# Interleaved attention and feed-forward on one core: the score tiles of VectorE moved, side work paused around them, six key tiles in column groups instead of eight

## The chip, the cores and the metric

The kernel runs on one core of a Trainium2 chip. The metric is the device time of one execution in microseconds (us). Before the change it is 2252.2 us, the median of three runs (2249.78 to 2252.49). Engines are named as in the profile: PE is the matrix engine, PEld its weight loads, DVE the vector engine, ACT the scalar engine, POOL GpSimd, SP the sync engine.

## What is computed

Two layers of attention and two of feed-forward, in turn, with the same weights in both rounds, on 2048 rows of 512 columns:

```python
x = x + _A_ref(_layernorm(x), A_wqkv, A_wo)
x = x + _B_ref(_layernorm(x), B_w1, B_w2)
x = x + _A_ref(_layernorm(x), A_wqkv, A_wo)
x = x + _B_ref(_layernorm(x), B_w1, B_w2)
```

`_A_ref` is full softmax attention with 32 heads of 16 dimensions: scores of 2048 by 2048 for each head, softmax over the keys, the weighted sum of the values, a product with `wo`. `_B_ref` is `silu(x @ w1) @ w2` with 1792 hidden columns. There is no mask, so every head needs all of its 4.2 million exponentials in each layer.

## The kernel before

**Units.** In a layer (`L`), the 2048 queries are four chunks of 512 (`c`), the 32 heads are eight groups of four (`hb`), and the 2048 keys are sixteen tiles of 128 (`kt`). One unit is (`c`, `hb`, `kt`): four heads, 512 queries, 128 keys. I call the sixteen units of one (`c`, `hb`) a block; a layer has 32 blocks, the kernel 64. PE, ACT and DVE each run in the order in which the program emits instructions; POOL and SP follow their own queues.

**What a unit emits** (lines 671 to 759). First the exponentials: a unit's scores lie in two PSUM tiles of 128 by 1024 (`s_ps`, two heads each, "pair 0" and "pair 1"), and ACT turns each into `p_sb` (line 686). Then PE gets the score products of the next unit (`emit_s`, four products of 32 rows that lie in different row groups, line 555). Then come the products of probabilities and values (`emit_pv`) that were put off by the unit before, then those of this unit's pair 0, and last the side work. The `s_ps` tiles are a ring of three, so a score product waits for the exponential three tiles back.

**Values in two forms.** For key tiles in `COL` the four heads' value products are 32 columns wide and go to four column groups (line 570). For the others, `DIAG`, each head's values lie in their own 32 of 128 columns of a zeroed tile `vd`, and four products of full width add up in `o_ps` (line 580). POOL fills the `vd` tiles, two key tiles at a time in a ring of two (`vd_fill`, line 151), from the value tensor `va`. Value products of a `COL` tile are put off whole to the next unit; of a `DIAG` tile, pair 1 is put off. At `kt` 0 both pairs are put off, because `o_ps` has one buffer and has to be emptied first (`finish_heads`, line 659, a DVE copy to `oT`).

**DVE's score tiles.** At key tiles in `OFF`, pair 1's exponential is made by DVE in seven passes (`exp_passes`, line 589). The first, `split` (line 601), reads the `s_ps` tile and is emitted in the unit itself; the other six are emitted one per unit in the following units. Until `split` has run, its `s_ps` tile isn't free. The value products of this pair are emitted seven units later (`late`).

**Side work.** Everything else is cut into steps that a queue (`Pump`) hands out at the end of a unit: for chunk 0 the key projections of the next head group (`k_piece`, steps a and b of two products each, four pieces, and `amax_bm`), for every block the query projection of the next block (`q_piece`, steps a, b, d) and the transposition of the finished heads (`heads_piece`), and for chunks 1 to 3 the previous chunk's output projection (`epilogue_pieces`: pa | pb, pc, four times), layer norm (`ln_steps`: statistics in two steps, then rs, then four transpositions tr), feed-forward (`ffn_pieces`: a, b, d for each of 14 hidden tiles, d being ACT's tanh with a DVE product; then 28 steps of the second product) and in layer 0 the next layer's layer norm and values (`next_pieces`). All side work on PE shares one PSUM buffer (`gpool`, one buffer, tile tag "g"): a step that opens a new tile waits until DVE has read the last one.

**How many steps.** Before the change a unit takes the queue's length, with a little for what the coming blocks will add, divided by the units left in the chunk, and rounded up; at least one while the next block's projections wait; none at `OFF` (lines 746 to 754). At `kt` 14 it takes as many as the next block's query needs. The number `left` is never set back, so in practice at least one step is taken in every unit up to `kt` 13 while the queue holds something.

**Ahead of the loop**: layer norm of all rows, the first projections, and on POOL the filling of constants: `va` is set to 1.0 throughout (line 142), because column 17 of each head must be one (it makes the softmax sum), and the weight columns are rearranged (line 125).

Of the kernel before, what the change touches and what calls it, by code (L numbers as in the profile page):

```python
# [18 lines left out]
def kernel(  # L19
# [10 lines left out]
    nc = tc.nc  # L30
# [15 lines left out]
    EPS = 1e-5  # L46
    VS = DH + 1
    NG = 2
    NR = 2

    COL = [1, 3, 5, 7, 9, 11, 13, 15]
    DIAG = [kt for kt in range(TT) if kt not in COL]

    KR = 32

    OFF = [1, 9]

    cpool = ctx.enter_context(tc.tile_pool(name="cpool", bufs=1))
    wpool = ctx.enter_context(tc.tile_pool(name="wpool", bufs=1))
# [57 lines left out]
    wkq = wpool.tile([P, CT, 2 * D + DH], BF16, name="wkq")  # L117
# [20 lines left out]
    VW = VS * H + 32 - VS  # L138
    vs = []
    for i in range(2):  # L140
        va = xpool.tile([P, TT, VW], BF16, name=f"va{i}")
        nc.gpsimd.memset(va[:], 1.0)
        vs.append(va)
    vdq = []
    for i in range(NR):
# [2 lines left out]
        vdq.append(vd)  # L148


    def vd_fill(va, hb, g, slot):
        k0, step = DIAG[NG * g], DIAG[1] - DIAG[0]
        for j in range(4):
            h = 4 * hb + j
            nc.gpsimd.tensor_copy(  # L155
                out=vdq[slot][:, :, j, 32 * j : 32 * j + VS],
                in_=va[:, k0 : k0 + step * (NG - 1) + 1 : step, VS * h : VS * h + VS],
            )


    def ln_stats(mvb, i, tt):
        st = small.tile([P, 6], FP32, name="st", tag="st")
# [110 lines left out]
    def amax_bm(hb):  # L273
        if OFF:
            ends = KT[64:P, hb, :].rearrange("p (k n) -> p k n", n=P)
# [266 lines left out]
    pump = Pump()  # L542
    state = {"begun": False}

    def pump_some(n):
        for _ in range(n):
            if not pump.q:
                return
            state["begun"] = pump.step()
# [11 lines left out]
            )  # L561
        return s_ps

    def emit_pv(o_ps, ps, hb, kt, prs, va):
        for pr in prs:
            for jj in range(2):
                j = 2 * pr + jj
                if kt in COL:
                    h = 4 * hb + j
                    nc.tensor.matmul(  # L570
                        o_ps[32 * j : 32 * j + 32, :],
                        lhsT=va[:, kt, VS * h : VS * h + 32],
                        rhs=ps[pr][:, jj, :],
                        start=False,
                        stop=(kt == TT - 1),
                        skip_group_check=True,
                    )
                else:
                    d = DIAG.index(kt)
                    nc.tensor.matmul(  # L580
                        o_ps[:, :],
                        lhsT=vdq[d // NG % NR][:, d % NG, j, :],
                        rhs=ps[pr][:, jj, :],
                        start=(kt == 0 and j == 0),
                        stop=False,
                        skip_group_check=True,
                    )
# [48 lines left out]
    for L in range(2):  # L636
        va = vs[L]
        last = L == 1
        QTs = [[None] * HB for _ in range(NQC)]
# [5 lines left out]
            for tt in range(0, TT, 2):  # L645
                v_two(xnTs[tt // 4], tt, va)
        for i in range(NR):
            vd_fill(va, 0, i, i)
# [8 lines left out]
        left = 0  # L657

        def finish_heads(o_ps, hb, attn):
            oT = opool.tile([P, 512], BF16, name="oT", tag="oT")  # L660
# [10 lines left out]
        for u, (c, hb, kt) in enumerate(units):  # L671
# [3 lines left out]
            off = kt in OFF  # L675

            ps = []
# [22 lines left out]
            if kt == 0:  # L700
                flush(u)
                assert not late
                if o_ps is not None:
                    finish_heads(o_ps, (hb - 1) % HB, attn)
                if hb == 0:
                    if c > 0:
                        pump.add(epilogue_pieces(c - 1, attn))
                        pump.add(ffn_pieces(c - 1, emit_out=last))
                        if not last:
                            pump.add(next_pieces(c - 1, nxt, vs[1]))  # L710
                    attn = new_attn
                o_ps = oppool.tile([P, 512], FP32, name="o_ps", tag="o")
                pend.append((o_ps, ps, hb, kt, (0, 1)))
                must = []
                if c == 0 and hb + 1 < HB:
                    must += [k_piece(xnTs, k, hb + 1) for k in range(NQC)]
                    must.append([lambda hb=hb: amax_bm(hb + 1)])
                if hb + 1 < HB:
                    must.append(q_piece(xnTs, c, hb + 1, QTs))
                elif c + 1 < NQC:  # L720
                    must.append(q_piece(xnTs, c + 1, 0, QTs))
                at = (1 if state["begun"] else 0) + (1 if u > 0 else 0)
                pump.q[at:at] = [list(p) for p in must]
                left = at + len(must)
            else:
                flush(u)
                if off:
                    s_now += [f() for f in nxt_s[1:]]
                    emit_pv(o_ps, ps, hb, kt, (0,), va)
                    late.append((u + 7, (o_ps, ps, hb, kt, (1,))))  # L730
                elif kt in COL:
                    pend.append((o_ps, ps, hb, kt, (0, 1)))
                else:
                    emit_pv(o_ps, ps, hb, kt, (0,), va)
                    pend.append((o_ps, ps, hb, kt, (1,)))
# [24 lines left out]
        flush(len(units) + TT)  # L760
        finish_heads(o_ps, HB - 1, attn)
# [36 lines left out]
```

## Time and profile before

| what | value |
|---|---|
| median of three runs | 2252.2 us |
| the profiled execution's own time | 2250.19 us |
| its span, first to last instruction | 2248.0 us |
| mean granted PE clock | 0.927 |
| PE, DVE, ACT, POOL busy | 1904.9, 1495.2, 1849.0, 354.5 us |
| exponentials on ACT (line 686) | 1920, busy 1806.0 us, idle 263.0 us before them |
| value products, full width (line 580) | 2048 |
| value products, column groups (line 570) | 1792 with `p_sb`, 256 with `pd_sb` |

A line of the instruction groups reads: source line, engine, operation, what it writes and reads with shapes, count, then busy time in us and the mean of one in ns, then the engine's idle time just before these instructions with what ended it. Times of single instructions overlap: ACT's exponentials last 1086 ns each but start 0.905 us apart when nothing holds them.

### The profile page before, as it was taken

Reading aid. Unit: us, or ns where it says so; the run is one execution under the profiler, and the core shown is the slowest. Engines: PE = TensorE matmul, PEld = TensorE weight load, DVE = VectorE, ACT = ScalarE, POOL = GpSimd, SP = SyncE. Lnnn points to the kernel's source line nnn. Section 1 sums busy time; section 2 is a strip of 40 time slices with the busy share of each in tenths; the row PEclk is TensorE's granted clock in tenths of the full one; section 3 lists DMA queues with packets and bytes.
Section 4 is the critical chain, followed back from the end, with each engine's and each line's share of the span. In section 5 each row is a group of like instructions: output and inputs, shape, how many; then the busy total and the mean of one; then the engine's idle time right before and its main releaser. Section 6 shows DMA issues by size and latency. Waiting matters only on the chain.

```text
span 2248.0 us, 29378 instructions
## 1 busy us (share of the span) xinstructions
PE 1904.9 (85%) x10560; PEld 590.5 (26%) x10560; DVE 1495.2 (67%) x2023; ACT 1849.0 (82%) x2024; POOL 354.5 (16%) x1048
## 2 busy tenths in 40 slices
PE   2989887888888987889867888898899888988896
PEld 1322222222222222222222222222223222322222
DVE  7676767666666666666745767667666766676664
ACT  0688887998789987999814888899999899999991
POOL 4111111121111211111100111112122121212210
PEclk9998899999899998999977989899999899999997
DMA  4000000000000000000000000000000000000000
GB/s 140 1 1 1 1 1 1 1 1 1 1 1 1 1 1 1 1 1 1 1 0 0 1 1 1 1 1 1 1 6 6 1 1 3 8 1 1 1 10 10
DMA packets 8481, 11.82 MB, mean 5 GB/s; under 512 B 400, under 2 KB 7312, under 8 KB 8336
## 3 DMA queue, kind: packets, MB, share of 16 engines
q1 hardware_dynamic: 7280, 8.39, 1.1%
q8 instruction: 82, 1.34, 0.3%
q10 hardware_dynamic: 1056, 1.57, 0.2%
q14 instruction: 63, 0.52, 0.1%
HBM read 7.86 MB, written 2.10 MB: 4 GB/s over the span
## 4 chain that ended last, share of the span: by engine, by line
PE 59%; ACT 18%; DVE 18%; issue 5%; DMA 0%; ACTq 0%; DVEq 0%
PE s_ps L555 19%; PE o_ps L580 17%; ACT p_sb L686 15%; PE o_ps L570 8%; PE y_ps L433 3%; PE h_ps L426 3%; DVE y L596 3%; PE k_ps L239 2%; ACT t_sb L463 2%; PE q_ps L327 2%; DVE st L163 2%; DVE amax L281 2%; PE y_ps L405 1%; DVE oT L661 1%; PE v_ps L290 1%
## 5 line engine op out<-in xcount | busy, mean ns | idle before, releaser
L686 ACT ACTIVATE p_sb<-s_ps 128x1024 bf16<-128x1024 f32 x1920 | 1806.0, 1086 | 263.0 <-PE s_ps L555 258.6
L555 PE MATMUL s_ps<-QT,KT 32*128 32x512 bf16 x4096 | 695.6, 400 | 140.0 <-ACT p_sb L686 113.9
L580 PE MATMUL o_ps<-p_sb,vd 128*128 128x512 bf16 x2048 | 645.6, 404 | 6.4 <-DVE oT L661 6.4
L155 POOL COPY vd<-va 128x34 bf16<-128x34 bf16 x1024 | 331.2, 337 | 1813.7 <-PE o_ps L580 1667.1
L555 PEld LDWEIGHTS <-KT 32*128 32x128 bf16 x4096 | 185.0, 91 | 777.7 <-issue 712.2
L596 DVE SCALAR_TENSOR_TENSOR y<-y,m 128x1024 f32<-128x1024 f32 x256 | 313.5, 1225 | 4.0
L570 PE MATMUL o_ps<-p_sb,va 128*32 128x512 bf16 x1792 | 215.4, 410 | 1.0 <-ACT p_sb L686 0.8
L580 PEld LDWEIGHTS <-vd 128*128 128x128 bf16 x2048 | 126.4, 99 | 272.6 <-issue 260.4
L601 DVE TENSOR_SCALAR z<-s_ps 128x1024 int32<-128x1024 f32 x128 | 155.9, 1218 | 21.6 <-PE s_ps L555 20.9
L596 DVE SCALAR_TENSOR_TENSOR pd_sb<-y,z 128x1024 bf16<-128x1024 f32 x128 | 158.4, 1237 | 3.7
L596 DVE SCALAR_TENSOR_TENSOR y<-m 128x1024 f32<-128x1024 f32 x128 | 156.0, 1219 | 0.0
L464 DVE SCALAR_TENSOR_TENSOR hT<-t_sb,h_ps 128x512 bf16<-128x512 f32 x84 | 57.6, 686 | 121.2 <-ACT t_sb L463 121.2
L661 DVE CAST oT<-o_ps 128x512 bf16<-128x512 f32 x64 | 44.3, 692 | 135.8 <-PE o_ps L570 135.8
L426 PE MATMUL h_ps<-xnT,w_sb 128*128 128x512 bf16 x448 | 130.6, 397 | 2.8 <-DVE hT L511 1.4
L433 PE MATMUL y_ps<-w_sb,hT 128*128 128x512 bf16 x448 | 123.8, 384 | 7.0 <-DVE hT L511 4.5
L208 PE MATMUL t_ps<-ident,xn 128*128 128x128 bf16 x256 | 34.8, 286 | 92.3 <-DVE xn L196 88.7
L342 DVE TENSOR_SCALAR qc<-q_ps,cols 128x512 bf16<-128x512 f32 x64 | 51.8, 809 | 84.8 <-PE q_ps L327 84.8
L256 DVE TENSOR_SCALAR KT<-k_ps,cols 128x512 bf16<-128x512 f32 x56 | 45.4, 810 | 92.0 <-PE k_ps L239 91.9
L327 PE MATMUL q_ps<-xnT,wkq 128*128 128x512 bf16 x256 | 79.6, 397 | 14.6 <-DVE attn L377 14.6
L607 DVE TENSOR_SCALAR m<-z 128x1024 int32<-128x1024 int32 x128 | 88.8, 694 | 4.4
L613 DVE TENSOR_SCALAR z<-z 128x1024 int32<-128x1024 int32 x128 | 88.1, 688 | 1.8
L570 PEld LDWEIGHTS <-va 128*32 128x32 bf16 x2048 | 55.0, 94 | 129.3 <-issue 129.0
(64 smaller groups left out, 998.2 us busy)
## 6 DMA issues: line engine op xcount, KB each, us to landing
w_sb<-in_B_w_dram SPq DMA_DIRECT2D x2, 1792.0 KB, 14.9
x_sb<-in_A_x_dram SPq DMA_DIRECT2D x4, 512.0 KB, 9.7
out_dram<-x_sb SPq DMA_DIRECT2D x16, 128.0 KB, 1.7
wraw<-in_A_wqkv_dram ACTq DMA_DIRECT2D x1, 1024.0 KB, 7.5
wv_sb<-in_A_wqkv_dram ACTq DMA_DIRECT2D x1, 512.0 KB, 10.0
wo_sb<-in_A_wo_dram SPq DMA_DIRECT2D x1, 512.0 KB, 11.9
```

The lines of the kernel that those rows point to most:

```text
L155: nc.gpsimd.tensor_copy(out=vdq[slot][:, :, j, 32 * j : 32 * j + VS], in_=va[:, k0 : k0 + step * (NG - 1) + 1 : step, VS * h : VS * h + VS],)
L327: nc.tensor.matmul(cell["ps"][:, :], lhsT=wkq[:, ct, P * hb + DH : P * hb + DH + P], rhs=xnTs[c][:, ct, :], start=(ct == 0), stop=(ct == C ...
L426: nc.tensor.matmul(ps, lhsT=w1_sb[:, ct, ft * P : (ft + 1) * P], rhs=xfT[:, ct, :], start=(ct == 0), stop=(ct == CT - 1),)
L433: nc.tensor.matmul(ps, lhsT=hT[:, ft, tq * P : (tq + 1) * P], rhs=w2_sb[:, ft, :], start=(ft == 0), stop=(ft == FT - 1),)
L555: nc.tensor.matmul(s_ps[:, jj, :], lhsT=KT[32 * j : 32 * j + KR, hb, kt * P : (kt + 1) * P], rhs=QT[32 * j : 32 * j + KR, :], start=True, ...
L570: nc.tensor.matmul(o_ps[32 * j : 32 * j + 32, :], lhsT=va[:, kt, VS * h : VS * h + 32], rhs=ps[pr][:, jj, :], start=False, stop=(kt == TT ...
L580: nc.tensor.matmul(o_ps[:, :], lhsT=vdq[d // NG % NR][:, d % NG, j, :], rhs=ps[pr][:, jj, :], start=(kt == 0 and j == 0), stop=False, skip ...
L596: nc.vector.scalar_tensor_tensor(out=out, in0=in0, scalar=POLY[k], in1=in1, op0=ALU.add, op1=ALU.mult)
L601: nc.vector.tensor_scalar(out=z[:], in0=s_ps[:].rearrange(flat), scalar1=-127.5 / (SCALE * LOG2E), scalar2=float(SCALE * LOG2E * 2**23), o ...
L607: nc.vector.tensor_scalar(out=m[:].bitcast(I32), in0=z[:], scalar1=0x7FFFFF, scalar2=0x3F800000, op0=ALU.bitwise_and, op1=ALU.bitwise_or,)
L613: nc.vector.tensor_scalar(out=z[:], in0=z[:], scalar1=0x40000000, scalar2=0x7F800000, op0=ALU.bitwise_xor, op1=ALU.bitwise_and,)
L686: nc.scalar.activation(p_sb[:].rearrange("p a b -> p (a b)"), s_now[pr][:].rearrange("p a b -> p (a b)"), ACT.Exp, scale=float(SCALE),)
```

## The change

- `COL` goes from the eight odd key tiles to `[2, 5, 7, 9, 12, 14]`, so `DIAG` has ten tiles, 0, 1, 3, 4, 6, 8, 10, 11, 13, 15, in five groups of two. `vd_fill` takes a running number of the group; the ring of two `vd` tiles stays.
- `OFF` goes from `[1, 9]` to `[2, 9]`.
- `REST` is the key tiles 0, 1, 2, 8, 9. There no side step is taken. Eleven of sixteen units take steps where fourteen did.
- The number of steps is reckoned over the units that are not in `REST`, with 4 steps (13 in chunk 0) for each coming block, and separately over the units up to `kt` 14 for the pieces that the next block needs (`due`); the larger counts. The rule of at least one step is gone.
- `va` is no longer filled whole: only the ones column of each head is set to 1.0, and the 15 columns of padding to 0.0. The weight columns are rearranged in another order of the same eight copies.

```diff
-    COL = [1, 3, 5, 7, 9, 11, 13, 15]
+    COL = [2, 5, 7, 9, 12, 14]
     DIAG = [kt for kt in range(TT) if kt not in COL]
+    GROUPS = [DIAG[i : i + NG] for i in range(0, len(DIAG), NG)]
 
-    OFF = [1, 9]
+    OFF = [2, 9]
+
+    REST = sorted({0} | {kt - 1 for kt in OFF} | set(OFF))
...
-    for ct in range(CT):
-        pairs = wkq[:, ct, 0 : 2 * D].rearrange("p (h t d) -> p h t d", t=2, d=DH)
-        for t in range(2):
+    for t in range(2):
+        for ct in range(CT):
+            pairs = wkq[:, ct, 0 : 2 * D].rearrange("p (h t d) -> p h t d", t=2, d=DH)
...
-        nc.gpsimd.memset(va[:], 1.0)
+        heads = va[:, :, 0 : VS * H].rearrange("p t (h s) -> p t h s", s=VS)
+        nc.gpsimd.memset(heads[:, :, :, DH:VS], 1.0)
+        nc.gpsimd.memset(va[:, :, VS * H : VW], 0.0)
...
-    def vd_fill(va, hb, g, slot):
-        k0, step = DIAG[NG * g], DIAG[1] - DIAG[0]
+    def vd_fill(va, at):
+
+        at_hb, g = divmod(at, len(GROUPS))
+        k0, k1 = GROUPS[g]
         for j in range(4):
-            h = 4 * hb + j
+            h = 4 * (at_hb % HB) + j
             nc.gpsimd.tensor_copy(
-                out=vdq[slot][:, :, j, 32 * j : 32 * j + VS],
-                in_=va[:, k0 : k0 + step * (NG - 1) + 1 : step, VS * h : VS * h + VS],
+                out=vdq[at % NR][:, :, j, 32 * j : 32 * j + VS],
+                in_=va[:, k0 : k1 + 1 : k1 - k0, VS * h : VS * h + VS],
             )
...
-                left = at + len(must)
+                due = pump.q[at + len(must) - 1] if must else None
...
-            nd = len(DIAG)
             if kt in DIAG and DIAG.index(kt) % NG == 0 and u > 0:
-                at_d = (c * HB + hb) * nd + DIAG.index(kt) + NG * (NR - 1)
-                if at_d < NQC * HB * nd:
-                    fhb, fd = at_d // nd % HB, at_d % nd
-                    vd_fill(va, fhb, fd // NG, fd // NG % NR)
-
-            remaining = TT * HB - (hb * TT + kt)
-            total = pump.steps()
-            later = sum(3 for _ in range(hb + 1, HB)) + (HB - 1 - hb)
-            todo = -(-(total + later) // remaining) if total else 0
-            if left and kt < TT - 2 and pump.q:
-                todo = max(todo, 1)
-            if off:
-                todo = 0
-            pump_some(todo)
+                at = (c * HB + hb) * len(GROUPS) + DIAG.index(kt) // NG + NR - 1
+                if at < NQC * HB * len(GROUPS):
+                    vd_fill(va, at)
+
+            if kt not in REST:
+                here = sum(1 for k in range(kt, TT) if k not in REST)
+                rest = here + (TT - len(REST)) * (HB - 1 - hb)
+                later = (HB - 1 - hb) * (4 + (9 if c == 0 else 0))
+                todo = -(-(pump.steps() + later) // rest) if pump.q else 0
+                where = [i for i, p in enumerate(pump.q) if p is due]
+                if where:
+                    steps = sum(len(p) for p in pump.q[: where[0] + 1])
+                    slots = sum(1 for k in range(kt, TT - 1) if k not in REST)
+                    todo = max(todo, -(-steps // max(slots, 1)))
+                pump_some(todo)
             if kt == TT - 2:
-
-                tgt_c, tgt_hb = (c, hb + 1) if hb + 1 < HB else (c + 1, 0)
-                while tgt_c < NQC and QTs[tgt_c][tgt_hb] is None:
+                while any(p is due for p in pump.q):
                     pump_some(1)
```

More of the change, by code (lines that the diff above doesn't have):

```diff
@@ L562, in emit_s, with emit_pv @@
         return s_ps
-    def emit_pv(o_ps, ps, hb, kt, prs, va):
+    def emit_pv(o_ps, ps, c, hb, kt, prs, va):
         for pr in prs:
@@ L578, in emit_pv @@
                 else:
-                    d = DIAG.index(kt)
+                    g, i = divmod(DIAG.index(kt), NG)
+                    at = (c * HB + hb) * len(GROUPS) + g
                     nc.tensor.matmul(
                         o_ps[:, :],
-                        lhsT=vdq[d // NG % NR][:, d % NG, j, :],
+                        lhsT=vdq[at % NR][:, i, j, :],
                         rhs=ps[pr][:, jj, :],
@@ L647 @@
         for i in range(NR):
-            vd_fill(va, 0, i, i)
+            vd_fill(va, i)
         nxt = [None] * NQC
@@ L656 @@
         s_now = [emit_s(QTs[0][0], 0, 0, pr) for pr in range(2)]
-        left = 0
+        due = None
         def finish_heads(o_ps, hb, attn):
@@ L712 @@
                 o_ps = oppool.tile([P, 512], FP32, name="o_ps", tag="o")
-                pend.append((o_ps, ps, hb, kt, (0, 1)))
+                pend.append((o_ps, ps, c, hb, kt, (0, 1)))
                 must = []
@@ L728 @@
                     s_now += [f() for f in nxt_s[1:]]
-                    emit_pv(o_ps, ps, hb, kt, (0,), va)
-                    late.append((u + 7, (o_ps, ps, hb, kt, (1,))))
+                    emit_pv(o_ps, ps, c, hb, kt, (0,), va)
+                    late.append((u + 7, (o_ps, ps, c, hb, kt, (1,))))
                 elif kt in COL:
-                    pend.append((o_ps, ps, hb, kt, (0, 1)))
+                    pend.append((o_ps, ps, c, hb, kt, (0, 1)))
                 else:
-                    emit_pv(o_ps, ps, hb, kt, (0,), va)
@@ L735 @@
-                    pend.append((o_ps, ps, hb, kt, (1,)))
+                    emit_pv(o_ps, ps, c, hb, kt, (0,), va)
+                    pend.append((o_ps, ps, c, hb, kt, (1,)))
             if passes and not off:
                 passes.pop(0)()
-            nd = len(DIAG)
             if kt in DIAG and DIAG.index(kt) % NG == 0 and u > 0:
-                at_d = (c * HB + hb) * nd + DIAG.index(kt) + NG * (NR - 1)
-                if at_d < NQC * HB * nd:
-                    fhb, fd = at_d // nd % HB, at_d % nd
-                    vd_fill(va, fhb, fd // NG, fd // NG % NR)
```

## The prediction

> **What bounds it now.** I read the page first.
>
> ```profile
> span 2248.0 us, 29378 instructions
> PE 1904.9 (85%) x10560; PEld 590.5 (26%) x10560; DVE 1495.2 (67%) x2023; ACT 1849.0 (82%) x2024; POOL 354.5 (16%) x1048
> ...
> L686 ACT ACTIVATE p_sb<-s_ps 128x1024 bf16<-128x1024 f32 x1920 | 1806.0, 1086 | 263.0 <-PE s_ps L555 258.6
> ...
> L155 POOL COPY vd<-va 128x34 bf16<-128x34 bf16 x1024 | 331.2, 337 | 1813.7 <-PE o_ps L580 1667.1
> ```
>
> ACT's exponentials are the floor, and the 258.6 us in which they waited for score products are all there is to win. In the timeline an undisturbed unit takes 1.81 us (two exponentials), a unit in `OFF` 0.905. A block's floor is 14 x 1.81 + 2 x 0.905 = 27.15 us; eight blocks, 217.2. The windows of the chunks (layer 0 chunks 0 and 1, layer 1 chunks 0 and 1; first number the length, last but two the PE clock):
>
> ```profile
> 73.50:329.60 256.10, 223.78 (x1198) 63.52 (x1198) 181.58 (x208) 223.49 (x241) 34.40 (x126) 0.91 0.00 1
> 329.60:592.00 262.40, 224.40 (x1290) 69.36 (x1288) 173.15 (x246) 231.43 (x256) 40.54 (x128) 0.95 0.00 1
> ...
> 1210.50:1470.00 259.50, 227.62 (x1199) 63.67 (x1193) 180.66 (x206) 223.79 (x240) 34.40 (x126) 0.88 0.00 1
> 1470.00:1710.00 240.00, 217.17 (x1256) 66.62 (x1254) 163.11 (x213) 229.59 (x255) 47.48 (x128) 0.96 0.01 3
> ```
>
> Above the floor: chunk 0, 38.9 and 42.3 us; chunks 1 to 3, 45.6 on average in layer 0 (45.2, 48.4, 43.2) but 22.8 in layer 1. Before each exponential I noted the wait. In a late block of chunk 0 (ACT alone, last figure the idle time before):
>
> ```profile
> 234.01 2.85 ACT L686 ACTIVATE p_sb<-s_ps 128x1024 bf16<-128x1024 f32 x3 [1.44 <-PE s_ps L555]
> 238.71 1.02 ACT L686 ACTIVATE p_sb<-s_ps 128x1024 bf16<-128x1024 f32 x1 [1.84 <-PE s_ps L555]
> 241.07 12.94 ACT L686 ACTIVATE p_sb<-s_ps 128x1024 bf16<-128x1024 f32 x14 [1.34 <-PE s_ps L555]
> 254.55 11.11 ACT L686 ACTIVATE p_sb<-s_ps 128x1024 bf16<-128x1024 f32 x12 [0.55 <-PE s_ps L555]
> ```
>
> The waits lie at the block's end (the query is late), at key tiles 1 and 2, and at 9. Units with one side step elsewhere wait for nothing. Layer 0's chunks 1 to 3 pay most in block 0, the one block whose units take two steps: 42.7, 46.8, 43.5 us against 32.1, 29.1, 29.1 in layer 1, where they take one.
>
> PE's prices at full clock, as distances of starts:
>
> ```profile
> 1220.51 0.40 PE L570 MATMUL o_ps<-p_sb,va 128*32 128x512 bf16 x4
> 1220.84 0.61 PE L580 MATMUL o_ps<-p_sb,vd 128*128 128x512 bf16 x2
> 1221.28 0.59 PE L239 MATMUL k_ps<-xnT,wkq 128*128 128x512 bf16 x2
> 1221.81 0.60 PE L555 MATMUL s_ps<-QT,KT 32*128 32x512 bf16 x4
> 1222.34 0.61 PE L580 MATMUL o_ps<-p_sb,vd 128*128 128x512 bf16 x2
> ```
>
> Column groups 0.33 us a key tile, full width 2 x 0.44 = 0.88, a unit's scores 0.53, a side step 0.44. A step that opens the shared PSUM tile after a step that DVE must still read waits (layer 0, chunk 1, block 0):
>
> ```profile
> 344.02 0.59 PE L405 MATMUL y_ps<-wo_sb,aT 128*128 128x512 bf16 x2
> 344.65 0.69 DVE L417 TENSOR_TENSOR x_sb<-x_sb,y_ps 128x512 bf16<-128x512 bf16 x1 [1.20 <-PE y_ps L405]
> 345.39 0.38 PE L396 MATMUL a_ps<-ident,attn 128*128 128x128 bf16 x4 [0.78 <-DVE x_sb L417]
> ```
>
> **The change, part by part.** Below, a unit's PE work is the sum of these prices; PE may run about 1.1 us late before ACT waits: a score product can start 1.1 us after a unit's first exponential, when the tile three back is free.
>
> *Key tiles at full width.* 64 blocks x 2 x (0.88 - 0.33) = 70 us more PE time. A block then needs 16 x 0.53 + 10 x 0.88 + 6 x 0.33 = 19.3 us and 0.44 per side step; with 11 steps 24.1, under the floor, so ACT covers it; with 22 steps 29.0, not covered: it is in the sums below. POOL makes 256 more `vd` copies (86 us at 337 ns); each fill has about three units (5.4 us) for four copies, and POOL idled 1813.7 us before them. If that cover failed, 1.3 us a fill would show.
>
> *`OFF` and rests.* An `OFF` unit lasts 0.905, so the next scores come late by what PE does between. At tile 9 with an unpumped tile 8 before it the trace has 0.36 (units where the queue was empty), with 0.97 us of value products between (0.33 + 0.20 + 0.44); with a step, 0.78 to 0.81. After, 0.77 us lies there: 0.15. At tile 2 it is 0.88 + 0.44 = 1.32: 0.36 + 0.35 = 0.7. Tile 1 costs nothing. So 0.9 a block where single steps suffice, for 1.7 to 3 now: the gain.
>
> *Where the steps go.* By the new formula chunk 0's blocks 1 to 5 take two steps at tiles 3 to 7 and 10, one at 11. Chunks 1 to 3 begin with 121 steps (layer 1) or 137 (layer 0) for 88 units; two a unit until 121 - 2n <= 88 - n: 33 units (three blocks), in layer 0 49 (four and a half). Then one.
>
> *Chunk 0, blocks 1 to 5.* [heads, k0a] at tile 3: the trace's [heads, qa] at tile 2 cost 0.52 to 0.55: 0.5. [k0b, k1a], [k1b, k2a], [k2b, k3a] at 4, 5, 6: each time PE waits for DVE's 0.81 us copy, about 0.9 by the 0.78 above. PE 0.53 + 0.88 + 0.88 + 0.9 = 3.2 at tile 4, 2.75 at 5, 3.1 at 6, less 1.81 each: 3.6, I take 3.3. Nearest rows, [pc, pa]: 0.65 to 1.75. Then `amax_bm` runs at tile 7, on DVE:
>
> ```profile
> 191.60 0.29 DVE L278 TENSOR_SCALAR KT<-KT,cols 64x256 bf16<-64x256 bf16 x1
> 191.93 2.29 DVE L281 TENSOR_REDUCE amax<-KT 128x1 f32<-128x2048 bf16 x1
> 194.25 0.25 DVE L285 TENSOR_SCALAR Bm<-E,amax 128x128 bf16<-128x128 bf16 x1
> ```
>
> Behind the last K copy come these 2.8 us, the pass of tile 8 (1.24) and only then `split` of tile 9 (1.22), which holds a score tile. In order: k3b ends 0.9 us after tile 8's first exponential; copy to 1.9, amax to 4.7, pass to 5.95, `split` to 7.2; scores 0.4: tile 11 starts at 7.7 instead of 4.7: 3.0. Before, amax lay at tile 11, far from a `split`. Bounds: 0 (DVE catches up) to 4.1 (all of amax and the pass). PE idles 3.2 us there. In this trace the clock fell to 0.50 behind smaller waits of PE (1.36 us for the query, at 199.74):
>
> ```profile
> 199.00:202.00 3.00, 2.27 (x14) 0.56 (x16) 1.81 (x3) 1.78 (x2) 0.52 (x2) 0.74 0.00 0
> 202.00:205.00 3.00, 2.21 (x13) 0.57 (x8) 1.34 (x4) 1.16 (x3) 0.00 (x0) 0.50 0.00 0
> ```
>
> so the two pumped units behind it (1.85 us of PE work each) run at half clock, each about 1 us over: 2.0 more (0 to 4). The block's-end wait (1.7) goes, the query being ready by tile 11. Sum 0.7 + 0.5 + 3.3 + 3.0 + 2.0 = 9.5 against 5.9 now. Block 0: 6 (no K waits); block 6 (amax at tile 10, after `split`): 4.7; block 7: 0.9. Chunk 0: 6 + 47.5 + 4.7 + 0.9 = 59; less 38.9 and 42.3: **+37**.
>
> [...]
>
> *Chunks 1 to 3.* Block 0: 0.7; [heads, qa] 0.6; [qb, qd] 1.5 (rows 0.82 to 2.38); output projection, [pa, pb] 0.6 and [pc, pa] 1.0 twice, 3.3; [rs, tr0] 5.0 (row 4.51; 0.7 us more of passes lie ahead on DVE); [tr1, tr2] 1.4 (row 1.36 to 1.78): 12.4, say 12. Blocks 1 and 2, feed-forward: [a, b], [d, a], [b, d]. In [b, d] tanh sits in ACT's queue behind a b just issued; the row at tile 10 is 1.16, of which 0.48 is tanh itself. In [d, a] PE waits for tanh and DVE's 0.69 and passes the delay to b. I take 1.2 per triple, 3.6 a block, beside tanh 0.48 each: 9.7 and 8.8 with heads, query and tile 2. Layer 0 then 5.7, 3.5 ([y, y] pairs cost 0.01 in their rows) and three times 0.9: 42.4 against 45.6, three times: **-10**. Layer 1 then 2.4 and four times 0.9: 36.5 against 22.8, three times: **+41**.
>
> *The rest.* Between the layers and at the tail the order is the same. The `va` fills were 15.3 us of POOL ahead of `vd`, while PE's and DVE's first work runs until 73.5 us; POOL waited 36.1 us for DVE there: 0, and no cost if slower, up to that wait.
>
> Sum 37 - 10 + 41 = 68. On the profiled execution's 2250.19: 2318; the median lies 2.0 higher: **2320 us**.
>
> **The rivals.**
> *Faster: the waits hide.* Some 186 units hold a PE wait inside a pair (4 in each of twelve chunk 0 blocks, about 25 in each other chunk of layer 0, 21 in layer 1). I price them near 0.9. If they cost 0.5 (lowest rows: 0.51, 0.52), -0.4 x 186 = -74: 2246. It decides below 0.55. For it: [st0, st1] and [a, b] cost nothing. Against: the ten other [pa, pb] and [pc, pa] units, 0.65 to 1.75.
> *amax meets no `split`.* 12 blocks x 5.0 = -60: 2260. For it: DVE is 70% busy in chunk 0's window. Against: its queue is in order.
> *Half clock spreads.* The chunk 0 windows already run at 0.88 to 0.91. Another 2 us in 12 blocks and 3 in six layer norms: +42, 2362.
>
> **How the numbers follow.** Chances: forecast 0.47, hiding 0.16, amax 0.19, clock 0.18. Runs before differ by 0.12%, so 0.2% (4.5 us) is about what a measurement can tell. Hiding gives faster, 0.16; amax at +8 splits 0.03 faster, 0.04 same; the rest is slower: 0.77. Range 2240 to 2375, from the hiding case to the clock case and its own error; the forecast's own is 2290 to 2350.
>
> **What would show it.** Right: waits at tiles 1 and 15 gone, tile 2 at 0.7, tile 9 at 0.15; in chunk 0 tile 10 three us over 1.81 with PE waiting for DVE `z`; layer 1's chunk windows at 250 to 257 us, layer 0's near 260, chunk 0's near 276. Wrong: layer 1's chunks below 240, or chunk 0 below 250: then two steps in a unit are cheaper than the rows say.

## The result, and the profile after

The changed kernel takes 2391.9 us (median of four runs, 2390.85 to 2395.55); the kernel before took 2251.1 us beside it. The ratio is 1.0628, with a 95% interval of 1.061 to 1.0647: 6.3% slower, 141 us. I had said 2320 us, with a range up to 2375. The sign was right, the size half of what came.

The page of the changed kernel (line 693 is now the exponentials, 587 the full-width value products):

```profile
span 2393.7 us, 29659 instructions
...
PE 1908.7 (80%) x10358; PEld 616.9 (26%) x10560; DVE 1496.1 (63%) x2023; ACT 1857.5 (78%) x2024; POOL 399.6 (17%) x1306
...
L693 ACT ACTIVATE p_sb<-s_ps 128x1024 bf16<-128x1024 f32 x1920 | 1804.5, 1061 | 329.9 <-PE s_ps L561 326.2
L587 PE MATMUL o_ps<-p_sb,vd 128*128 128x512 bf16 x2405 | 726.6, 396 | 27.3 <-issue 19.1
```

Busy times moved little: ACT 1849.0 to 1857.5 us, PE 1904.9 to 1908.7. (This trace lacks 202 of PE's 10560 products, 155 of them at full width; that of experiment 1, with the same forms of products, has them all and 1927.8 us.) What grew is waiting. The list of waits, changed kernel first (engine and line, what it waited for, total us, times, longest):

```profile
ACT p_sb L693 <- PE s_ps L561: 326.2, 265, 44.6
...
ACT t_sb L469 <- PE h_ps L432: 70.3, 34, 4.4
```

and the second of these in the kernel before:

```profile
ACT t_sb L463 <- PE h_ps L426: 5.7, 12, 0.5
```

ACT's wait for scores went from 258.6 to 326.2 us, 68 more. Its wait for the input of tanh went from 5.7 to 70.3, and 6.5 more are put down to a value product: 71 more. Together that is 139 of the 145.7 us by which the span grew.

The windows of the chunks (layer 0 chunks 0 and 1, layer 1 chunks 0 and 1; length first), to be read against 256.1, 262.4, 259.5 and 240.0 before. Layer 0's chunk 1 itself runs from 350.8 to 626.9 us and lasts 276.1, as long as the window in the second line:

```profile
68.40:350.80 282.40, 225.32 (x1174) 66.44 (x1198) 182.25 (x208) 226.14 (x241) 46.29 (x156) 0.91 0.00 1
356.00:632.00 276.00, 227.44 (x1270) 73.27 (x1294) 175.19 (x248) 231.58 (x254) 49.62 (x161) 0.94 0.00 1
...
1259.00:1542.00 283.00, 224.69 (x1175) 66.49 (x1191) 181.37 (x206) 225.68 (x240) 45.27 (x156) 0.91 0.00 1
1542.00:1806.00 264.00, 220.56 (x1237) 70.85 (x1260) 164.38 (x213) 231.09 (x256) 48.18 (x160) 0.96 0.01 2
```

By blocks, from the starts of the exponentials in the timeline (us; six chunks where chunks 1 to 3 are meant):

| block | before | predicted | after |
|---|---|---|---|
| chunk 0, block 0 | 28.2, 30.2 | 33.2 | 36.1, 36.8 |
| chunk 0, blocks 1 to 5 | 31.0 to 33.8 | 36.65 | 36.1 to 37.8 |
| chunk 0, block 6 | 33.0, 33.8 | 31.9 | 33.3, 32.3 |
| chunks 1 to 3, block 0 | layer 0 42.7 to 46.8, layer 1 29.1 to 32.1 | 39.2 | 39.9 to 44.8 |
| chunks 1 to 3, block 1 | 30.2 to 32.6 | 36.9 | 41.7 to 43.5 |
| chunks 1 to 3, block 2 | 30.4 to 32.2 | 36.0 | 36.9 to 38.4 |
| single steps throughout (layer 1, blocks 4 to 7) | 28.6 to 30.6 | 28.05 | 28.3 |

The gain that the change brings is in the last row: a block whose units take one step each falls to 28.3 us, 1.1 above the floor. The loss is where units now take two steps and took one before: chunk 0's blocks 0 to 5, blocks 1 and 2 of the other chunks, and block 0 of those in layer 1.

**The place in chunk 0.** Timeline of the changed kernel, layer 0, chunk 0, block 3 (start, length, engine; idle time before it in brackets). Tile 8's first exponential starts at 197.17.

```profile
196.15 0.59 PE L245 MATMUL k_ps<-xnT,wkq 128*128 128x512 bf16 x2 [0.90 <-DVE KT L262]
...
199.25 2.29 DVE L287 TENSOR_REDUCE amax<-KT 128x1 f32<-128x2048 bf16 x1
...
201.74 1.22 DVE L603 SCALAR_TENSOR_TENSOR pd_sb<-y,z 128x1024 bf16<-128x1024 f32 x1
203.01 0.61 PE L576 MATMUL o_ps<-pd_sb,va 128*32 128x512 bf16 x2 [2.65 <-DVE pd_sb L603]
...
203.55 0.60 PE L561 MATMUL s_ps<-QT,KT 32*128 32x512 bf16 x2
...
204.26 2.10 ACT L693 ACTIVATE p_sb<-s_ps 128x1024 bf16<-128x1024 f32 x2 [3.31 <-PE s_ps L561]
```

The first line is the wait inside [k2b, k3a], 0.90 us, as priced. The others show amax ahead of tile 8's pass; PE stands 2.65 us for these probabilities; the scores behind them in PE's queue come late; ACT waits 3.31 us. I had expected the delay, but from another wait: that of `split`, one instruction later on DVE. The clock follows (windows of 3 us, clock third from the end):

```profile
202.00:205.00 3.00, 1.99 (x10) 0.42 (x9) 2.86 (x3) 0.74 (x1) 0.00 (x0) 0.51 0.00 0
205.00:208.00 3.00, 3.00 (x14) 0.83 (x10) 0.06 (x2) 2.22 (x3) 0.00 (x0) 0.50 0.00 0
```

**The place that I priced too low.** Layer 1, chunk 1, block 2: tile 5 takes the query's last step d and the first of a hidden tile, tile 6 takes b and tanh.

```profile
1638.01 1.23 DVE L603 SCALAR_TENSOR_TENSOR y<-m 128x1024 f32<-128x1024 f32 x1
1638.15 0.38 PE L361 MATMUL q_ps<-qu,Bm 128*128 128x512 bf16 x1 [0.37 <-DVE qu L354]
1639.17 0.68 DVE L365 TENSOR_TENSOR QT<-q_ps,qc 128x512 bf16<-128x512 f32 x1
...
1639.89 0.38 PE L432 MATMUL h_ps<-xnT,w_sb 128*128 128x512 bf16 x1 [1.37 <-DVE QT L365]
...
1640.42 0.40 PE L561 MATMUL s_ps<-QT,KT 32*128 32x512 bf16 x4
...
1641.52 0.59 PE L432 MATMUL h_ps<-xnT,w_sb 128*128 128x512 bf16 x2
...
1642.15 0.60 ACT L469 ACTIVATE t_sb<-h_ps 128x512 f32<-128x512 f32 x1 [2.87 <-PE h_ps L432]
```

The query's sum waits on DVE behind a pass (1.23 us) that was emitted earlier; PE waits 1.37 us for it; everything behind is late; and ACT, which runs in order, stands 2.87 us at a tanh, although the scores of the next unit are there since 1640.8 (line 561).

### The profile page after: what moved, and what is told of

Read it like the earlier page. It is cut to its first block, busy times and chain, and to the rows that moved or that the text cites. A ratio compares the mean times of both kernels' runs of the same rounds, so it can differ in the third digit from the quotient of the medians.

```text
span 2393.7 us, 29659 instructions
## 1 busy us (share of the span) xinstructions
PE 1908.7 (80%) x10358; PEld 616.9 (26%) x10560; DVE 1496.1 (63%) x2023; ACT 1857.5 (78%) x2024; POOL 399.6 (17%) x1306
## 4 chain that ended last, share of the span: by engine, by line
PE 58%; ACT 18%; DVE 17%; issue 5%; another core or an unknown queue 1%; DMA 0%; ACTq 0%; DVEq 0%
PE o_ps L587 20%; PE s_ps L561 16%; ACT p_sb L693 16%; PE o_ps L576 6%; PE h_ps L432 3%; PE k_ps L245 3%; PE y_ps L439 3%; DVE y L603 2%; PE q_ps L333 2%; ACT t_sb L469 2%; DVE KT L262 2%; DVE st L169 1%; PE y_ps L411 1%; DVE amax L287 1%
## 5 line engine op out<-in xcount | busy, mean ns | idle before, releaser
L693 ACT ACTIVATE p_sb<-s_ps 128x1024 bf16<-128x1024 f32 x1920 | 1804.5, 1061 | 329.9 <-PE s_ps L561 326.2
L587 PE MATMUL o_ps<-p_sb,vd 128*128 128x512 bf16 x2405 | 726.6, 396 | 27.3 <-issue 19.1
L561 PE MATMUL s_ps<-QT,KT 32*128 32x512 bf16 x4096 | 639.8, 398 | 133.3 <-ACT p_sb L693 121.5
L162 POOL COPY vd<-va 128x34 bf16<-128x34 bf16 x1280 | 386.8, 315 | 1914.6 <-PE o_ps L587 1659.6
L561 PEld LDWEIGHTS <-KT 32*128 32x128 bf16 x4096 | 166.0, 91 | 708.7 <-issue 689.6
L587 PEld LDWEIGHTS <-vd 128*128 128x128 bf16 x2560 | 171.9, 99 | 320.6 <-issue 257.6
L432 PE MATMUL h_ps<-xnT,w_sb 128*128 128x512 bf16 x426 | 123.6, 404 | 47.7 <-DVE hT L470 25.1
L576 PE MATMUL o_ps<-p_sb,va 128*32 128x512 bf16 x1280 | 159.4, 407 | 0.0
L469 ACT ACTIVATE t_sb<-h_ps 128x512 f32<-128x512 f32 x84 | 51.2, 610 | 76.7 <-PE h_ps L432 70.3
L245 PE MATMUL k_ps<-xnT,wkq 128*128 128x512 bf16 x253 | 75.5, 394 | 42.6 <-DVE KT L262 32.5
L445 DVE SCALAR_TENSOR_TENSOR x_sb<-y_ps,x_sb 128x512 bf16<-128x512 f32 x32 | 22.1, 692 | 127.4 <-PE y_ps L439 127.4
```

Of the source, the lines that this page charges most:

```text
L162: nc.gpsimd.tensor_copy(out=vdq[at % NR][:, :, j, 32 * j : 32 * j + VS], in_=va[:, k0 : k1 + 1 : k1 - k0, VS * h : VS * h + VS],)
L245: nc.tensor.matmul(ps, lhsT=wkq[:, ct, P * hb : P * hb + P], rhs=xnT[:, ct, :], start=(ct == 0), stop=(ct == CT - 1),)
L432: nc.tensor.matmul(ps, lhsT=w1_sb[:, ct, ft * P : (ft + 1) * P], rhs=xfT[:, ct, :], start=(ct == 0), stop=(ct == CT - 1),)
L469: nc.scalar.activation(t_sb[:], hc["ps"][:, :], ACT.Tanh, scale=0.5)
L561: nc.tensor.matmul(s_ps[:, jj, :], lhsT=KT[32 * j : 32 * j + KR, hb, kt * P : (kt + 1) * P], rhs=QT[32 * j : 32 * j + KR, :], start=True, ...
L576: nc.tensor.matmul(o_ps[32 * j : 32 * j + 32, :], lhsT=va[:, kt, VS * h : VS * h + 32], rhs=ps[pr][:, jj, :], start=False, stop=(kt == TT ...
```

## The experiments

All times are medians; "of before" is the ratio to the kernel before, run beside it, with its interval. The edits are against the changed kernel unless another is named.

**1. The old number of steps.** The lines of the old planner in place of the new, `left` for `due`, so that no tile rests but 2 and 9.

```diff
-            if kt not in REST:
-                here = sum(1 for k in range(kt, TT) if k not in REST)
...
+            remaining = TT * HB - (hb * TT + kt)
+            total = pump.steps()
+            later = sum(3 for _ in range(hb + 1, HB)) + (HB - 1 - hb)
+            todo = -(-(total + later) // remaining) if total else 0
+            if left and kt < TT - 2 and pump.q:
+                todo = max(todo, 1)
+            if off:
+                todo = 0
+            pump_some(todo)
```

> The changed kernel with the number of side steps reckoned as before the change (one a unit in most blocks, none in the two units in OFF alone); six column tiles, OFF at 2 and 9 and the ones set alone stay. Theory (the loss sits in units that take two side steps): a block with single steps lasts 28.3 us in the changed kernel's trace; a step at tiles 1 and 8 adds 0.43 each, 29.1; chunk 0 has the late query again, 1.7 more. Chunk 0 near 245 us, layer 0's other chunks near 255, layer 1's near 236: 2190 us (2170 to 2225). Rival (the 70 us of PE time for two more tiles at full width are the loss): above 2320. In no case between would one of them alone do.

Measured: 2246.6 us, 0.9997 of before (0.9976 to 1.0017). All of the loss is gone, with ten key tiles still at full width: the rival fails. But nothing is gained either, where I had expected 60 us. In chunk 0 tile 1 still costs 0.8 us over the floor, tile 2 2.2 and tile 15 1.3, about what tiles 1, 2 and 15 cost before: side work at tiles 0 and 1 makes the short unit's scores late wherever the short unit is, and the query is late at the block's end. Moving `OFF`, with six column tiles and the short fill of `va`, gains nothing by itself.

**2. The rests and the new number alone**, on the kernel before.

```diff
     OFF = [1, 9]
+    REST = sorted({0} | {kt - 1 for kt in OFF} | set(OFF))
...
+            if kt not in REST:
+                here = sum(1 for k in range(kt, TT) if k not in REST)
...
```

> The kernel before with the new count of side steps and the rests alone (OFF stays at 1 and 9, so the rests are tiles 0, 1, 8, 9; eight column tiles; ones set as before). Theory: the count does nearly all of it: 25 units of two steps at the head of each chunk of layer 1 (none before), 41 in layer 0 (some 10 before), pairs in chunk 0 with amax at tile 6: layer 1's chunks 16 us longer each, layer 0's 8, chunk 0 8: 2340 us (2310 to 2375). Rival (moving OFF and the column tiles is the loss): below 2270.

Measured: 2331.2 us, 1.0337 of before (1.0321 to 1.0353). As expected: the planner alone makes the kernel 3.4% slower. Layer 1's chunks 1 to 3 are 16 to 18 us longer, chunk 0 8 to 10, layer 0's others 0 to 4. The two halves don't add up to the whole, though: 0 and 3.4% against 6.3%. Some 65 us come only where they meet.

**3. Eight column tiles** with everything else as changed.

```diff
-    COL = [2, 5, 7, 9, 12, 14]
+    COL = [2, 4, 5, 7, 9, 11, 12, 14]
```

> The changed kernel with key tiles 4 and 11 in column groups too, so eight again; rests, rate and OFF as changed. Theory (two-step units): PE has 0.55 us less at two tiles of a block, which counts where PE is late, about 0.8 us in 12 blocks of chunk 0 and 1 us in some 24 others: 2360 us (2345 to 2378). Rival (full-width tiles are the loss): 70 us or more come off, 2320 or below.

Measured: 2360.9 us, 1.0505 of before (1.0481 to 1.0529), 31 us less than the changed kernel, where I had written 2360. Full width costs where PE is already late from pairs, and that is about half of the 65 us.

**4. Four rests instead of five**, with eight column tiles, to find the other half.

```diff
-    REST = sorted({0} | {kt - 1 for kt in OFF} | set(OFF))
+    REST = sorted({0, OFF[1] - 1} | set(OFF))
```

> The changed kernel with eight column tiles, and tile 1 not rested: rests at 0, 2, 8, 9, so twelve units take steps, as in the run with the new count and the rests on the kernel before (2331 us), which differs from this one in having OFF at 1 and the odd tiles in column groups. With five rests this kernel took 2361 us. Theory (what the five rests add is the longer stretch of two-step units, 33 and 49 units instead of 25 and 41, and amax one tile later): about 2335 us (2320 to 2348). Rival (moving OFF from 1 to 2 costs the 30 us by itself): 2355 or more.

Measured: 2364.5 us, 1.05 of before (1.0471 to 1.053): no less than experiment 3. My expectation failed and the rival's number came, but the run has a cause of its own for it. Its trace shows two effects that cancel: block 2 of layer 1's chunk 2 falls from 36.1 to 32.9 us, as fewer units take two steps, while the pair now taken at tile 1 stands ahead of the short tile 2. Tiles 1 and 2 together cost 2.3 us over their floor in chunk 0 and 1.8 in the other chunks, against 0.9 to 1.0 with five rests.

So no run separates the causes of the other 34 us, but the traces of experiments 2 and 3 show where most of them lie. Experiment 3's chunks are longer than experiment 2's by 37 us in all: 18 in the two chunks 0, nearly all of it at tiles 8 to 11, where the wait behind amax falls; 13 in layer 1's others, where block 2 takes two steps a unit only with the five rests (36.1 to 37.6 us against 30.0); and 5 in layer 0's others.

**5. amax behind the `split` of tile 9.** The step is held until tile 10.

```diff
+                held = pump.q[at + NQC] if c == 0 and hb + 1 < HB else None
...
-                pump_some(todo)
+                for _ in range(todo):
+                    if kt < 10 and pump.q and pump.q[0] is held:
+                        break
+                    pump_some(1)
```

> The changed kernel with the amax step of chunk 0 held back to tile 10 or later, behind the split of tile 9; nothing else moves but the steps behind it. Theory (amax runs into tile 9's passes on DVE): tile 10 falls from 5.4 to about 2.1 us and tile 11 from 3.2 to about 2 in ten blocks, and the two blocks 0 lose 5 us each: about 55 us less, 2337 us (2325 to 2350). Rival (tile 10 is slow for PE's half clock, which other waits set off): under 20 us less, above 2372.

Measured: 2353.0 us, 1.0468 of before (1.0445 to 1.0491), 39 us less. In chunk 0 tile 10 fell from 4.49 to 2.10 us and tile 11 from 2.94 to 1.81, as the theory has it. But the query's steps now fall together behind it, [qb, qd], and tile 12 rose from 1.92 to 3.22, 21 us in sixteen blocks: more than the 16 us by which the run missed. The half clock largely went with that wait: the granted clock of the chunk 0 windows is 0.96 and 0.95, where the changed kernel has 0.91 in both.

**6. The late value product one unit later**, at tile 10 instead of 9. Which of DVE's two outputs is in the way?

```diff
-                    late.append((u + 7, (o_ps, ps, c, hb, kt, (1,))))
+                    late.append((u + (8 if kt == OFF[0] else 7), (o_ps, ps, c, hb, kt, (1,))))
```

> The changed kernel with the value products of DVE's pair of tile 2 emitted eight units later, at tile 10, instead of seven, at tile 9. In the changed kernel's trace PE waits 2.65 us at tile 9 for these probabilities, before it can make tile 10's second scores; I had expected the wait one tile on, for split to free its score tile. Theory (both waits hang on the same DVE queue behind amax): tile 10 falls to about 2.1 us and tile 11 rises by about 3, the total within 12 us of the changed kernel: 2380 to 2400. Rival (the value product alone is in the way): 25 us or more less, below 2367.

Measured: 2348.5 us, 1.0416 of before (1.0399 to 1.0434), 43 us less. The rival holds, and my account of the `split` was wrong. Layer 0, chunk 0, block 3 of this run:

```profile
189.07 0.39 PE L561 MATMUL s_ps<-QT,KT 32*128 32x512 bf16 x2
...
189.99 0.39 PE L561 MATMUL s_ps<-QT,KT 32*128 32x512 bf16 x2 [0.52 <-ACT p_sb L693]
191.09 0.39 PE L576 MATMUL o_ps<-pd_sb,va 128*32 128x512 bf16 x2 [0.71 <-DVE pd_sb L603]
191.14 1.23 DVE L608 TENSOR_SCALAR z<-s_ps 128x1024 int32<-128x1024 f32 x1
```

The scores of tile 11 are made at 189.07 and 189.99, before `split` (line 608) has even begun at 191.14: they took the other two score tiles, each right behind an exponential. So the tiles are not used in a strict turn of three, as the description of the kernel and the prediction have it: a score product doesn't wait for the tile three back when another is free. This `split` held nobody up; the product that needs DVE's finished probabilities did. Tile 10 also lost 0.3 us in every block, 28.0 instead of 28.3: the late product stood between the two score products of a short unit's successor.

**7. tanh not in the unit of its own product.**

```diff
+            d.apart = True
             pieces.append([a, b, d])
...
-                pump_some(todo)
+                for i in range(todo):
+                    if i and pump.q and hasattr(pump.q[0][0], "apart"):
+                        break
+                    pump_some(1)
```

> The changed kernel, where a unit stops before a feed-forward step d (tanh on ACT) if it has already taken another step, so that tanh never stands in ACT's queue behind a product issued in the same unit. Theory (ACT is held by tanh): the pair [b, d] costs 2.1 us beyond tanh's own 0.48 at 39 places, 83 us; some comes back, as the queue lasts longer and more units take two steps: 2340 us (2310 to 2365). Rival (PE's own waits inside the pairs set the time, ACT's wait at tanh only shows them): within 15 us of the changed kernel, above 2377.

Measured: 2356.9 us, 1.0484 of before (1.0461 to 1.0507), 35 us less. ACT's wait at tanh is gone:

```profile
ACT t_sb L469 <- PE h_ps L432: 2.6, 7, 0.4
```

Of 74 us of waiting, 35 came off the end. Block 1 of layer 1's chunk 1 fell from 42.1 to 37.8 us and block 2 from 36.9 to 32.3, but block 3 rose from 29.8 to 33.1, as the queue lasts a block longer. ACT held by tanh is a cause and no mere sign; the return of part of it was expected, and was larger.

**8. Pairs that don't wait.** The same rests, `OFF` and six column tiles, but the steps cut anew.

```diff
-        return [a, b]
+        return [joined(a, b)]
...
-        return [a, b, d]
+        return [joined(a, b), d]
...
-            pieces += [[pa], [pb, pc]]
+            pieces += [[pa], [joined(pb, pc)]]
...
-            pieces.append([a, b, d])
+            pieces.append([joined(a, b), d])
...
+            pieces.append([joined(*y[:3]), joined(*y[3:5]), joined(*y[5:])])
...
-                later = (HB - 1 - hb) * (4 + (9 if c == 0 else 0))
+                later = (HB - 1 - hb) * (3 + (5 if c == 0 else 0))
```

(`joined` runs its steps one after the other; the hold of experiment 5 is in it too.)

> The changed kernel (six column tiles, OFF 2 and 9, the same rests), with the side work cut anew: steps whose pairs cost nothing in the traces are joined (both halves of a k, v or hidden-tile product; query a and b; pb and pc; the two layer norm statistics; second-product steps 3, 2 and 2), and a unit takes one joined step; amax waits for tile 10; an empty step stands behind rs in layer 1. So no pair opens the side PSUM tile behind a DVE read, and tanh never stands behind its own product in a unit. Theory (which steps share a unit, not how many products, costs the time): blocks near 28.3 us plus tanh and 0.2 for joined products: chunk 0 near 230 us, layer 0's other chunks near 240, layer 1's near 235: 2120 us (2090 to 2170). Rival (the rests squeeze PE's work into eleven units, or the two full-width tiles do, whatever is paired): above 2230.

Measured: 2177.3 us, 0.9655 of before (0.9641 to 0.9669): 215 us less than the changed kernel, with side work in the same eleven units of a block, and faster than the kernel before. What shares a unit decides; holding amax, which is part of this edit, was worth 39 us by itself in experiment 5. The run missed 2120 by 57 us and the range by 7. Some 34 of the 57 lie where the layer norm stands: its statistics and rs fell on tiles 6 and 7 and delayed DVE's last pass just as amax had, and tile 10 cost 6.0 us over its floor in six blocks, where other blocks have 0.3.

**9. Eight column tiles with these pairs.** The edit of experiment 3 on experiment 8.

> The kernel with joined steps with key tiles 4 and 11 in column groups too, so eight. Theory: PE is not late where one joined step is taken, so 0.55 us less at two tiles of a block hides under ACT: 0 to 15 us less than with six. Rival (two tiles at full width cost their 70 us of PE time): 40 us less or more.

Measured: 2168.1 us, 0.9609 of before (0.9591 to 0.9627), 9 us less than with six. The full-width products of the two runs, six column tiles and then eight:

```profile
L597 PE MATMUL o_ps<-p_sb,vd 128*128 128x512 bf16 x2560 | 751.0, 392 | 10.1 <-DVE oT L679 7.1 <-ACT p_sb L704 1.5
```

```profile
L597 PE MATMUL o_ps<-p_sb,vd 128*128 128x512 bf16 x2048 | 630.6, 402 | 11.1 <-DVE oT L679 8.9 <-ACT p_sb L704 0.7
```

The 512 full-width products with their 120 us of busy time gave way to as many in column groups (PE's whole busy time fell from 1873.8 to 1846.0 us; by the prediction's prices the exchange is 70). It gained 9 us. Where PE isn't late, ACT covers nearly all of it, as the prediction's first part had it.

**10. No rests but at `OFF`**, with these pairs and eight column tiles.

```diff
-    REST = sorted({0} | {kt - 1 for kt in OFF} | set(OFF))
+    REST = sorted(OFF)
```

> The kernel with joined steps and eight column tiles, with rests only at the tiles of OFF, 2 and 9, so that side work is taken at tiles 0, 1 and 8 again. Theory (side work ahead of a short unit makes the next scores late: heads at tile 0 wait for DVE's copy of o_ps, 0.8 us, a joined product at tile 1 or 8 adds 0.4 to 0.9): 1.2 us a block, 77 us more than with the rests: 2245 us (2215 to 2270). Rival (the rests do nothing once the pairs are right): within 15 us of it, below 2185.

Measured: 2260.2 us, 1.0037 of before (1.0024 to 1.005). The rests are worth 92 us once the pairs are right. On the means of the chunks 0, layer 0's others and layer 1's others, tile 2 costs 1.8 to 2.1 us over its floor, tile 1 0.6 to 1.2 and tile 0 0 to 0.65; with the rests tile 2 costs 0.7 to 1.5 and the other two at most 0.15.

**11. The late product later, and the statistics kept away**, on experiment 9.

```diff
-                    late.append((u + 7, (o_ps, ps, c, hb, kt, (1,))))
+                    late.append((u + (8 if kt == OFF[0] else 7), (o_ps, ps, c, hb, kt, (1,))))
...
+        both.long = True
...
+                    if kt not in (3, 4, 10, 11, 12) and pump.q and hasattr(pump.q[0][0], "long"):
+                        break
```

> The kernel with joined steps and eight column tiles, with two things more: the value products of DVE's pair of tile 2 come eight units later, not seven, and the two joined layer norm statistics are taken only at tiles 3, 4, 10, 11 and 12, away from DVE's passes that those products need. Theory: the late product cost 0.29 us at tile 10 in every block (18 us) and 5.5 us where the statistics stood at tile 7 (6 places, some 20 to 25 us): 2128 us (2110 to 2150). Rival (DVE is behind as much, and another wait follows): above 2155.

Measured: 2144.8 us, 0.953 of before (0.9517 to 0.9543), the fastest of the study, 4.7% below the kernel before and 247 us below the changed one. Its windows, the same four chunks:

```profile
65.60:301.80 236.20, 206.13 (x1175) 62.39 (x1198) 180.54 (x208) 223.48 (x240) 43.96 (x124) 0.92 0.00 1
301.80:549.70 247.90, 212.97 (x1265) 69.23 (x1288) 172.37 (x244) 229.39 (x255) 43.54 (x128) 0.95 0.00 1
...
1132.30:1363.90 231.60, 200.95 (x1175) 62.35 (x1195) 179.84 (x206) 222.65 (x240) 45.06 (x124) 0.97 0.00 1
1363.90:1602.60 238.70, 210.05 (x1236) 68.78 (x1256) 163.83 (x214) 229.48 (x256) 49.39 (x128) 0.97 0.01 3
```

It is 17 us above what I expected of it, within the bounds. Some 14 of these lie in block 1 of layer 0's chunks 1 to 3. There the statistics and rs share tile 10, tr0 and tr1 share tile 11, and tile 12 costs 4.6 us over its floor; in layer 1, where rs and tr0 have units of their own and an empty step lies between them, tile 12 costs nothing extra.

**12. The ones alone**, on the kernel before: only the value tensor's ones and padding are set, and the weight copies come in the new order.

```diff
-        nc.gpsimd.memset(va[:], 1.0)
+        heads = va[:, :, 0 : VS * H].rearrange("p t (h s) -> p t h s", s=VS)
+        nc.gpsimd.memset(heads[:, :, :, DH:VS], 1.0)
+        nc.gpsimd.memset(va[:, :, VS * H : VW], 0.0)
```

> The kernel before with the ones column and the padding of the value tensor set alone, and the weight copies in the new order; nothing else. Both theories: 0, within 0.2% of the kernel before, since POOL fills the tensor ahead of the loop while PE and DVE work on the layer norm.

Measured: 2244.8 us, 0.997 of before (0.9959 to 0.998). Both theories missed: this part gains about 6 us. The first exponential starts at 65.4 us instead of 73.5. Timelines, before and then this run:

```profile
12.88 15.32 POOL L142 MEMSET va<- 128x8944 bf16 x2
...
13.33 7.38 DVE L196 TENSOR_SCALAR xn<-x_sb,mvb,rstd 128x512 bf16<-128x512 bf16 x1
```

```profile
13.03 2.42 POOL L143 MEMSET va<- 128x512 bf16 x1
...
13.48 2.32 DVE L198 TENSOR_SCALAR xn<-x_sb,mvb,rstd 128x512 bf16<-128x512 bf16 x1
```

One normalization of 128 by 512 on DVE lasted 7.38 us; it ends at 20.71, and POOL's first fill (12.88 plus 7.69) at 20.57. With the short fill the same instruction lasts 2.32, and with no fill beside it 0.40. Two more, begun beside the second long fill, took 3.77 us together. The weight copies took 4.63 us in both runs, so their new order isn't the cause.

## Why the prediction was right or wrong

- **What bounds the kernel, and the direction**: right. Experiments 1, 2 and 8 show that neither the full-width products nor the moved `OFF` make it slower by themselves, but the units that take two steps.
- **Rests**: right for a block of single steps, 0.72 us at tile 2 and 0.06 to 0.16 at tile 9 where I had 0.7 and 0.15. Not seen: the late product's 0.3 at tile 10, about 19 us in 64 blocks.
- **Full-width tiles**: hidden under ACT as said where single joined steps are taken (9 us of the 70 that the prices give), but 31 us where pairs already make PE late.
- **Chunk 0, blocks 1 to 5**: right in size, 36.1 to 37.8 for 36.65. K pairs 1.42, 0.98 and 1.31 us, 3.7 for my 3.3; tiles 10 and 11 together 5.0 for 3.0 and 2.0. Wrong in one link: "`split` of tile 9 (1.22), which holds a score tile" held nothing; the late product waits for the pass before it (experiment 6). That the sum came out is luck in this link: the two waits stand one instruction apart on DVE. Block 0, which I priced at 6, costs 9 to 9.6: the same wait, and a longer stretch of half clock (0.50 from 90 to 99 us in layer 0). With block 6, the two chunks 0 missed by 13 us.
- **Block 0 of chunks 1 to 3**: 41.2 on average for 39.2, 12 us. Its terms add up to 12.4 or 12.5, of which I took 12, and [rs, tr0] costs 6.05, not 5.0.
- **The step that failed** is the feed-forward's: "I take 1.2 per triple, 3.6 a block". [b, d] costs 2.61 us with tanh's own 0.48, so 2.1, over 39 places, and in all 3.5 to 5.0 where it follows [qd, a] or [tr3, a] (a, b, d are the steps of a hidden tile). So the feed-forward's units cost 9.0 us in each of the blocks 1 and 2, tanh included, where the sum had 6.0 to 6.5 (3.6, and 0.48 five or six times): some 33 us too little in twelve blocks. I priced each pair as if the unit before it ended on time, and left out DVE's passes, which stand between the query's parts. The mechanism was named, the size of its term was off by nearly half. In block 2 the query's pairs hide most of it, 0.25 us where I had 2.1, and the block is only 1.1 above its price.
- **The wait behind the layer norm**: block 1 came out 5.4 us above its price in each of six chunks, 33 us. The feed-forward is 3 of that. Another 3.1 lie at its tiles 0 to 2, before any feed-forward step. They follow [tr1, tr2], which I had put at 1.4 in block 0 and which costs 1.78 at the next block's tile 0; 1.3 more at tiles 1 and 2, at a granted clock of 0.50 (1580 to 1589 us in layer 1's chunk 1), were in the sum at nothing. Other terms of the block came out a little below their price.
- **The ones**: "0, and no cost if slower" looked for POOL's waiters and not at DVE's own 7.38 us in the same stretch, which the chain of waits shows. The changed kernel starts its loop at 68.4 us instead of 73.5.
- **The rivals**: none came. The waits inside pairs didn't hide. amax met the late product instead of the `split`, and cost about what I had said. The half clock didn't spread: the mean granted clock rose from 0.927 to 0.934. I had no case in which the pairs together cost more than their prices one by one, so the range ended too low. The misses by block, 13, 12, 33 and some 7 for block 2, 4 for block 3 and 10 for the single-step blocks, less 5 ahead of the loop, come to 74, near the 72 us between 2320 and 2392.
- **Open**: half of the 65 us by which the whole exceeds its parts; experiment 4 says where most of it lies, but no run separates its causes.

## What to carry to other kernels

When work is interleaved by hand, count what waits inside a slot, not only how much work is in it: here two steps that share one buffer (PE stood 0.90 us inside [k2b, k3a], 1.37 us behind the query's sum) and an ACT instruction behind a product of the same slot (ACT stood 2.87 us at a tanh) cost a round trip each, and the next slot inherited it. The rests that cost the kernel before 3.4% with the new count (experiment 2) are worth 92 us once steps are joined so that pairs don't wait (experiment 10). And when one engine's long instruction is moved, ask which in-order queue reads the output that is behind it: here it was a put-off product on PE, and putting it off by one more unit gave back 43 us.

## What the hardware showed unexpectedly

A fill on POOL stretched a DVE instruction from 0.40 to 7.38 us, nearly as long as the fill ran (7.69), in data that had nothing to do with it (experiment 12). The fill began first (12.88 against 13.33 us), and the instruction ends 0.14 us after it. Not every DVE instruction was stretched: beside the second long fill, which ends at 28.20 us, the statistics of 128 by 512 (line 163) lasted 0.66 to 0.69 us each (21.75 to 24.82 us), and 0.66 to 0.68 with no fill beside them, from 32.11 us on. Why the one was stretched and the other was not, no run shows.

PE's clock fell to half within a wait of 2.65 us. In this wait of the changed kernel, which ends at 203.01, the granted clock is 1.00 until 202.0, 1.7 us after PE's last product ended, and 0.50 from 202.5 to 208.5. In the kernel before, it was 0.50 from 200.5 on, behind the wait of 1.36 us that ended at 199.74; in the changed kernel it stayed at 1.00 behind one of 1.37 us, which ended at 1639.89. So the length of the wait alone doesn't decide here, and what does was not shown. With the wait at 203.01 moved or gone (experiments 5 and 6) the windows of chunk 0 have 0.95 to 0.97 instead of 0.91, and the mean granted clock of the whole run is 0.943 to 0.949 instead of 0.934 to 0.937. What part of the 2.0 us that I priced at tiles 10 and 11 is the clock alone was not measured apart.
